# Loading q, k and v as f32 from SP's hardware queue and rounding them to bf16 by copies on Pool, in a dilated sliding-window attention with soft mixture of experts

## The chip, the cores and the metric

One core of one Trainium2 chip runs the whole kernel. The metric is the device time of one launch in microseconds (us). Engines are named as in the profile: PE (TensorE), PEld (its weight loads), DVE (VectorE), ACT (ScalarE), POOL (GpSimd), SP (SyncE, which only issues DMAs here). Fewer microseconds are better.

## The reference

Eight batches (B = 8) of eight heads (H = 8), 576 positions (S), head width 64 (D). The first four heads of a batch look back over the last 32 positions, the other four over the last 128 at every fourth position. The result, 4608 tokens of width 512, goes through a soft mixture of experts with 8 experts of 4 slots each.

```python
scores = scale * np.matmul(q, k.transpose(0, 1, 3, 2))
mask_plain = (rel >= 0) & (rel < 32)
mask_dil   = (rel >= 0) & (rel < 32 * 4) & (rel % 4 == 0)
attn = softmax(np.where(masks, scores, -1e9))          # rows
x = (attn @ v) as (4608, 512)
logits = x @ phi                                       # (4608, 32)
d = softmax(logits over tokens); slot_input = d.T @ x  # (32, 512)
slot_out[e] = relu(slot_input[e] @ w1[e]) @ w2[e]      # w1[e] 512x1024, w2[e] 1024x512
out = softmax(logits over slots) @ slot_out            # (4608, 512)
```

q, k, v, the weights and the output are f32 in HBM; the kernel computes in bf16 with f32 sums.

## The kernel before, in words

**Units.** The work is cut into 16 units n (`NSU`): one batch and one half of its heads, even units the plain window, odd units the dilated one. Each unit takes three loads, k, q and v of four heads (w = 3n, 3n + 1, 3n + 2), 48 loads in all, each 128 partitions by 1152 elements. A unit runs through stages: `stage_T` (L632) transposes k, q and v on PE (L640 in even units, L643 in odd ones) and ACT or DVE copies them out of PSUM into `seq`, in the tile `aren` (helper `cp`, L330 for ACT, L331 for DVE); `stage_V` (L656) transposes blocks of v (L672); `stage_S` (L687) puts the mask into PSUM by a matmul (L695, L698) and adds the scores (L704); `stage_P` (L714) takes row maxima on DVE (L723), splits them into a bf16 head and a bf16 rest by a small subtraction on DVE (L725), subtracts both on PE (L732), takes exp on ACT (L738) and transposes (L745); `stage_O` (L754) multiplies with v (L766) and divides (L776, L778); `stage_X` (L782) transposes the result (L796). Every second unit `gating` (L810) adds a batch to the gate's running sums.

**Loads.** `load(w)` (L472) brings one load in two halves of 64 partitions (`NPQ = 2`). The DMAs are issued on Pool's software queue (L485) and round f32 to bf16 on their way. They land in a ring of 9 slots (`NSLOT`, 1152 elements each) in the tile `stg_all`; load w goes into slot w mod 9, and so can't start before the transposes of load w - 9 are done. Pool's queue also issues the weights (`load_w`, L489, L504): w1 and w2 of the 8 experts in four pieces each, 64 DMAs, rounded on their way too. Six experts' w2 have a place of their own (`N_W2R = 6`, tile `w2b`); experts 6 and 7 reuse `stg_all` when its slots are done. phi comes on SP's hardware queue (L553), and so does the output at the end (L1132, 19 DMAs). Pool has little else: selects that build the identity (L513), the masks (L524, L527, L547) and the group mask `mskg` (L584, L588) in the first 25 us.

**After the units.** The gate's sums are closed (L998 to L1020), `slot_input` is formed (L1022, L1030), the first layer runs (`first_layer`, L1037, matmuls L1043), the hidden values are transposed (L1062), the second layer runs (`second_layer`, L1070, matmuls L1076), and then 36 blocks of the output are multiplied (L1117), copied (L1125 on ACT, L1126 on DVE) and stored.

**What sets the order.** Every operation is given to a planner (`Prog`): with the engines that may run it and a cost in us, what it reads and writes (`Buf`) and a priority (`P.cur`). `schedule` (L161) goes through time by those costs: of the operations ready on an engine it takes the one of best priority, and it picks ACT or DVE where both may do. The order so found is fixed for each engine, and `emit` (L242) writes it out with semaphore waits where an operation needs another engine's result (or, on Pool, always the operation before it). So a changed cost or engine changes the whole order. An operation marked `paced` (most loads, all weights) waits, besides, for the landing of an earlier load, so chosen that about 3 us of transfers (`COVER`) stand ahead of it. Loads of unit n + 3 get priority 100n - 100, weights 1700 (a lower number goes first).

```python
for n in range(NSU):
    P.cur = 100 * n - 60
    stage_T(n)
    P.cur = 100 * n - 100
    for w in range(3 * n + NSLOT, min(3 * n + NSLOT + 3, 3 * NSU)):
        load(w)
```

Of the kernel before, what the change touches and what calls it, by code (L numbers as in the profile page):

```python
# [19 lines left out]
LSEQ = 2 * S  # L20
# [82 lines left out]
class Op:  # L103
    __slots__ = ("opts", "fn", "raw", "war", "prio", "rounds", "eng", "start", "end",
                 "sem", "val", "clock", "hard", "mm", "bytes", "dsem", "nleft", "users", "idx", "waits", "paced",
                 "more")


class Prog:
# [12 lines left out]
    def op(self, opts, fn, r=(), w=(), a=(), rounds=(), prio=None, dma=None, extra=(), hard=(), mm=1,  # L122
           paced=False):
        o = Op()
        o.paced = paced
        o.mm = mm
        o.more = self.more
        o.idx = len(self.ops)
        o.opts, o.fn = opts, fn
        o.prio = self.cur if prio is None else prio  # L130
        o.rounds = list(rounds)
        o.bytes, o.dsem = dma if dma else (0, None)
        raw, war = set(extra) | set(hard), set()
        o.hard = set(hard)
        for b in r:
            raw.update(b.w)
        for b in a:
            war.update(b.prev)
        for b in w:
            raw.update(b.w)  # L140
            war.update(b.prev)
            war.update(b.r)
        for b in r:
            b.r.append(o)
        for b in a:
            b.w.append(o)
        for b in w:
            b.prev = b.w + b.r
            b.w, b.r = [o], []
        for rd in o.rounds:  # L150
            rd.ops.append(o)
            if len(rd.ops) > 1:
                raw.update(rd.ops[:-1])
        raw.discard(o)
        war.discard(o)
        o.raw, o.war = raw, war - raw
        o.eng = None
        self.ops.append(o)
        return o

    def schedule(self):  # L161
# [22 lines left out]
        while ready:  # L184
# [43 lines left out]
            if o.bytes:  # L228
                dma_free = max(dma_free, o.end + 1.3) + o.bytes / 400e3
                o.end = dma_free + 0.4  # L230
                if e == "POOL":
                    loads.append((o, o.bytes / 400e3))
# [9 lines left out]
    def emit(self, nc, blk):  # L242
# [6 lines left out]
        for o in self.order:  # L249
# [7 lines left out]
            for d in o.war:  # L257
                if d.dsem is None and d.eng == e:
                    continue
                need.append(d)  # L260
# [73 lines left out]
def bass_dilated_sliding_attn__then__soft_moe_slots_kernel(  # L334
# [16 lines left out]

    NSLOT = 9
    SLOT = 1152
    w1b = sb("w1b", [128, E_EXP, 4, FF])
    N_W2R = 6
    w2b = sb("w2b", [128, N_W2R, 8, DM])
    stg_all = sb("stg_all", [128, NSLOT * SLOT])
    slots = [stg_all[:, SLOT * i:SLOT * (i + 1)] for i in range(NSLOT)]
    VW = 18 * 2 * 66
# [44 lines left out]

    sm_all = stg_all[:, 8192:9408].bitcast(F32)
    sab = sm_all[:, 0:256].bitcast(BF16)
# [19 lines left out]

    b_stg = [Buf() for _ in range(NSLOT)]
    b_seq = [[Buf() for _ in range(3)] for _ in range(2)]
    b_VOV = [Buf() for _ in range(2)]
# [22 lines left out]
    NPQ, NPW = 2, 4  # L452
    s_stg = [[nc.alloc_semaphore(f"s_stg{i}_{j}") for j in range(NPQ)] for i in range(NSLOT)]
    s_w1 = [[nc.alloc_semaphore(f"s_w1_{e}_{j}") for j in range(NPW)] for e in range(E_EXP)]
# [17 lines left out]
    def load(w, paced=True):  # L472
        n, t = w // 3, w % 3
        b, ty = su_bt(n)
        i = w % NSLOT
        hs = (k, q, v)[t][b, 4 * ty:4 * ty + 4]
        if ty == 0:
            dst = slots[i].rearrange("p (h c) -> p h c", h=2)
            ap = hs.rearrange("(p x) (i c) d -> (x i) p (c d)", p=2, c=9)
        else:  # L480
            dst, ap = slots[i], hs.rearrange("h (i c) d -> (h i) (c d)", c=18)
        m = 128 // NPQ
        for j in range(NPQ):
            sl = slice(m * j, m * j + m)
            P.op(POOL, lambda g, sl=sl: g.dma_start(dst[sl], ap[sl]),  # L485
                 dma=(m * LSEQ * 5, s_stg[i][j]), paced=paced,
                 **(dict(w=[b_stg[i]]) if j == 0 else dict(a=[b_stg[i]])))

    def load_w(kk, e):  # L489
# [6 lines left out]
        for i in range(n_p):  # L496
# [4 lines left out]
            else:  # L501
                sl = (slice(m * i, m * i + m), slice(0, c))
                bw = b_w
            P.op(POOL, lambda g, sl=sl: g.dma_start(dst[sl], ap[sl]), paced=True,  # L504
                 dma=(4 * DM * FF // n_p, sem[i]),
# [4 lines left out]
    small(lambda vv: vv.memset(ident[:], 0.0), w=[b_ident])  # L510
    for w in range(3):
        load(w, False)
    pool(lambda g: g.affine_select(  # L513
        out=ident[:], in_=ident[:], compare_op=AluOp.not_equal, fill=1.0, base=0,
        pattern=[[-1, 128]], channel_multiplier=1), w=[b_ident], r=[b_ident])

    for w in (3, 4):
        load(w, False)
    for i in range(2):
# [10 lines left out]
    for j in range(1, 4):  # L530
        small(lambda vv, j=j: vv.tensor_copy(mbase[32 * j:32 * j + 32, :], mbase[0:32, :]),
              w=[b_mb], r=[b_mb])
    for w in range(5, NSLOT):
        load(w)
    small(lambda vv: vv.tensor_scalar(idneg[:], ident[:], -1.0, None, op0=AluOp.mult),
# [414 lines left out]
    for n in range(NSU):  # L950
        P.more = P.DVE_MORE if n < NSU - 1 else 0.0
        P.cur = 100 * n - 60
        stage_T(n)
        P.cur = 100 * n - 100
        for w in range(3 * n + NSLOT, min(3 * n + NSLOT + 3, 3 * NSU)):
# [17 lines left out]
    P.more = 0.0  # L973
    stg_of = lambda c0, c1: [b_stg[i] for i in range(c0 // SLOT, min((c1 - 1) // SLOT + 1, NSLOT))]
    for i, e in enumerate(range(N_W2R, E_EXP)):
# [13 lines left out]
    for nb in (b_sab, b_siT, b_rep, b_frow):  # L989
        for bb in stg_of(8192, 9408):  # L990
            nb.r += bb.all_ops()
# [189 lines left out]
```

## Time and profile before

| | |
|---|---|
| median of 3 runs | 234.81 us (234.13 to 240.28) |
| the profiled execution, its own time | 232.67 us |
| its span, first to last instruction | 230.9 us |
| mean granted TensorE clock | 0.901 |
| first transposes of k | 5.59 us |
| loads of q, k, v issued | 1.3 to 134.8 us |
| weights issued | 48.7 to 196.4 us |
| first layer's matmuls begin | 191.15 us |
| output stores issued | 204.4 to 224.4 us |

A line of the page's first part gives an engine's busy time, its share of the span and its instructions. In the groups and in the timeline, "out<-in" names the tiles; "idle before" in square brackets is how long the engine had nothing to do and what ended that. The waits add such idle times up by who waited for whom: total us, times, longest. The chain is followed back from the last instruction, at each step to what released it. A PE that is busy is not a PE at its peak, since matmuls overlap; the granted clock is the share of the full TensorE clock in that stretch.

```
stretch (us)   PE busy  DVE busy  ACT busy  POOL busy  granted clock  DMA share
12 to 20        7.71      3.89      5.39      6.79        1.00          1.02
20 to 40       16.17     14.53     12.39     11.18        1.00          0.96
60 to 80       18.14     13.12     11.54      7.39        0.85          0.87
120 to 140     17.32     13.71     11.88      8.44        0.91          0.96
160 to 180     15.49     11.68      8.52      6.54        0.83          0.98
190 to 200      9.16      4.76      0.00      2.66        0.72          0.99
207 to 231      9.41     13.38      8.48      0.00        0.76          0.92
```

### The profile page before, as it was taken

The numbers are of one execution on the slowest core, as the hardware profiler recorded it, in microseconds if no ns is written. First come the engines' busy times: TensorE is split into PE (matmuls) and PEld (weight loads), VectorE is DVE, ScalarE is ACT, GpSimd is POOL, SyncE is SP. The second block draws the span as 40 slices with busy tenths as digits, with TensorE's granted clock in tenths as the row PEclk, the third lists the DMA queues.
The fourth block names the chain that finished last, engine by engine and source line by source line (L and its number), as shares of the span: only waits on it lengthen the run. The fifth ranks groups of instructions, "written<-read, shape, count | busy, mean of one in ns | idle before, by whom it ended". The sixth has DMA issues, their size and how long they took to land.

```text
span 230.9 us, 9919 instructions
## 1 busy us (share of the span) xinstructions
PE 181.4 (79%) x4502; PEld 123.9 (54%) x4502; DVE 145.5 (63%) x322; ACT 121.9 (53%) x190; POOL 89.3 (39%) x187
## 2 busy tenths in 40 slices
PE   0699597996999899899789979698969479984810
PEld 0476476665767568566556657366744343442300
DVE  3356586788547667677785676728772463468750
ACT  2557665864538779674685748264634120073640
POOL 7687564434506444542544343233341333000000
PEclk9999999999779999999997999979985755999785
DMA  6999998799987999999989899979999899849996
GB/s 85 179 142 163 156 153 124 112 163 137 157 170 101 148 168 162 150 161 173 158 136 174 165 168 160 189 136 193 186 183 193 138 169 177 143 177 406 397 408 253
DMA packets 17562, 41.08 MB, mean 178 GB/s; under 512 B 3440, under 2 KB 9584, under 8 KB 15600
## 3 DMA queue, kind: packets, MB, share of 16 engines
q0 software_dynamic: 14208, 30.94, 80.9%
q1 hardware_dynamic: 3312, 9.50, 10.6%
q8 instruction: 35, 0.57, 1.0%
q14 instruction: 7, 0.06, 0.1%
HBM read 61.93 MB, written 9.44 MB: 309 GB/s over the span
## 4 chain that ended last, share of the span: by engine, by line
PE 64%; DVE 12%; issue 8%; ACT 6%; DMA 5%; POOL 1%; SPq 0%; DVEq 0%; POOLq 0%
PE ps L672 9%; PE ps L732 7%; PE ps L640 6%; PE ps L704 5%; PE ps L766 4%; PE ps L745 4%; PE ps L796 4%; PE ps L695 4%; PE ps L643 4%; DVE aren L331 3%; DMA out_dram<-aren 3%; DVE aren L1126 3%; PE ps L1043 3%; DMA stg_all<-in_v_dram 2%; ACT aren L330 2%
## 5 line engine op out<-in xcount | busy, mean ns | idle before, releaser
L330 ACT ACTIVATE aren<-ps 128x1152 bf16<-128x1152 bf16 (+2 forms) x49 | 53.0, 1099 | 34.0 <-PE ps L640 12.4
L331 DVE COPY aren<-ps 128x1152 bf16<-128x1152 bf16 (+2 forms) x31 | 34.2, 1113 | 10.9 <-PE ps L640 4.7
L723 DVE TENSOR_REDUCE nm<-ps 128x10 f32<-128x640 f32 (+1 forms) x32 | 24.1, 753 | 7.1 <-PE ps L704 6.8
L504 POOL DMA_DIRECT2D w1b<-in_moe_w_dram x32 | 15.9, 497 | 27.3 <-DMA w1b<-in_moe_w_dram 10.0
L485 POOL DMA_DIRECT2D stg_all<-in_k_dram x32 | 17.9, 562 | 21.6 <-PE ps L640 12.6
L778 DVE TENSOR_TENSOR xn<-ps,rv 128x576 bf16<-128x576 f32 x32 | 24.2, 758 | 1.1
L640 PE MATMUL ps<-ident,stg_all 128*64 128x128 bf16 x432 | 18.4, 243 | 7.5 <-DMA stg_all<-in_k_dram 5.6
L672 PE MATMUL ps<-ident,aren 128*128 128x128 bf16 (+1 forms) x304 | 22.7, 232 | 1.8 <-issue 1.5
L485 POOL DMA_DIRECT2D stg_all<-in_v_dram x32 | 17.7, 558 | 14.4 <-DMA stg_all<-in_k_dram 5.3
L330 ACT ACTIVATE xt<-ps 128x640 bf16<-128x640 bf16 (+1 forms) x21 | 13.2, 661 | 18.9 <-PE ps L796 18.8
L738 ACT ACTIVATE pp<-ps 128x640 bf16<-128x640 f32 (+1 forms) x32 | 20.0, 654 | 4.7 <-PE ps L732 4.2
L766 PE MATMUL ps<-aren,pp 64*32 64x65 bf16 x1152 | 15.2, 194 | 8.8 <-issue 6.7
L504 POOL DMA_DIRECT2D w2b<-in_moe_w_dram x24 | 11.7, 489 | 26.3 <-DMA w2b<-in_moe_w_dram 22.1
L485 POOL DMA_DIRECT2D stg_all<-in_q_dram x32 | 17.7, 560 | 9.9 <-PE ps L643 3.0
L640 PEld LDWEIGHTS ps<-ident,stg_all 128*64 128x64 bf16 x432 | 15.1, 124 | 11.1 <-POOL ident L513 5.6
L672 PEld LDWEIGHTS ps<-ident,aren 128*128 128x128 bf16 (+1 forms) x304 | 18.3, 105 | 3.4 <-issue 1.8
L704 PE MATMUL ps<-aren 64*32 64x64 bf16 x1152 | 15.7, 196 | 3.7 <-issue 3.7
L704 PEld LDWEIGHTS ps<-aren 64*32 64x32 bf16 x1152 | 11.5, 95 | 12.5 <-issue 12.5
L766 PEld LDWEIGHTS ps<-aren,pp 64*32 64x32 bf16 x1152 | 10.9, 92 | 13.2 <-issue 7.6
L643 PE MATMUL ps<-ident,stg_all 128*128 128x128 bf16 x216 | 16.4, 223 | 2.0 <-issue 1.6
L732 PE MATMUL ps<-nm,idneg 128*128 128x512 bf16 (+1 forms) x48 | 16.4, 352 | 0.1
L643 PEld LDWEIGHTS ps<-ident,stg_all 128*128 128x128 bf16 x216 | 13.2, 100 | 4.6 <-issue 1.9
(143 smaller groups left out, 311.4 us busy)
## 6 DMA issues: line engine op xcount, KB each, us to landing
out_dram<-aren SPq DMA_DIRECT2D x17, 512.0 KB, 5.6
w1b<-in_moe_w_dram POOLq DMA_DIRECT2D x32, 256.0 KB, 5.6
w2b<-in_moe_w_dram POOLq DMA_DIRECT2D x24, 256.0 KB, 5.6
stg_all<-in_k_dram POOLq DMA_DIRECT2D x32, 144.0 KB, 4.3
stg_all<-in_q_dram POOLq DMA_DIRECT2D x32, 144.0 KB, 4.7
stg_all<-in_v_dram POOLq DMA_DIRECT2D x32, 144.0 KB, 4.7
stg_all<-in_moe_w_dram POOLq DMA_DIRECT2D x8, 256.0 KB, 5.5
out_dram<-aren SPq DMA_DIRECT2D x2, 256.0 KB, 2.3
```

The costliest lines, as they stand in the source:

```text
L330: return eng.activation(dst, src, ACTF.Copy)
L331: return eng.tensor_copy(dst, src)
L485: P.op(POOL, lambda g, sl=sl: g.dma_start(dst[sl], ap[sl]), dma=(m * LSEQ * 5, s_stg[i][j]), paced=paced, **(dict(w=[b_stg[i]]) if j == 0 ...
L504: P.op(POOL, lambda g, sl=sl: g.dma_start(dst[sl], ap[sl]), paced=True, dma=(4 * DM * FF // n_p, sem[i]), **(dict(w=[bw]) if i == 0 or bw ...
L640: ins = pe_.transpose(rd.h[64 * p:64 * p + 64, oc], sl[:, 576 * p + 64 * c:576 * p + 64 * c + 64], ident[:])
L643: ins = pe_.transpose(rd.h[:, oc], sl[:, oc], ident[:])
L672: ins = pe_.transpose(rd.h[row:row + nk, 128 * i:128 * i + 128], seq[u][:, 2, sl], ident[:])
L704: ins = pe_.matmul(rd.f[32 * j:32 * j + 32, 64 * (tile - t0):64 * (tile - t0) + 64], qk(u, p_, k, j, 1, 32, 0), qk(u, p_, k, j, 0, 64, 1), ...
L723: P.op([dve(ne)], lambda vv, sv=sv, nv=nv: vv.tensor_reduce(nv, sv(), AXX, AluOp.max), rounds=[rd], w=[b_nm[u][i]])
L732: ins = pe_.matmul(rd.f[:, 64 * a:64 * b], idneg[:], m[:, a:b].unsqueeze(2).to_broadcast([128, b - a, 64]), start=False, stop=True, skip_g ...
L766: ins = pe_.matmul(rd.f[32 * oq:32 * oq + 32, 103 * pl:103 * pl + 65], pt[u][sl, tile // 2, 32 * j:32 * j + 32], VOV[u][sl, pv, j % 2 if u ...
L778: P.op([dve(576)], lambda vv, cols=cols, rvp=rvp, p=p: vv.tensor_tensor(xn[x][:, :, p, :], cols(0, 64), rvp.unsqueeze(2).to_broadcast([128 ...
```

## The change

The 96 half loads of q, k and v are issued on SP's hardware queue. They are not rounded on their way: they land as f32 in a ring of 5 f32 slots (`NFS`, load w in slot w mod 5). A copy on Pool for each load (48, given to the planner at 1.2 us) rounds it into one of 4 bf16 slots (load w in slot w mod 4), which `stage_T` reads as before. A load waits for the copy of load w - 5, a copy for its load and for the transposes of load w - 4. The weights stay on Pool's queue and are still rounded on their way; they are issued among the copies. `stg_all` grows from 9 x 1152 to 14 x 1152 elements of two bytes, and `w2b` shrinks from 6 experts to 5, so that experts 5, 6 and 7 reuse `stg_all` at the end. The loads' priority becomes 100n - 200, and only the first 4 loads stand ahead of the loop in the program. The order of every engine is planned anew. On SP the first six half loads stand ahead of phi's four DMAs. On Pool the order at the start is: a weight issue, the select for the identity, a weight issue, two selects for `mbase`, two for `mask`, the first copy, five selects, the second copy, a select, the third copy.

```diff
-    NSLOT = 9
+    NSLOT, NFS = 4, 5
     SLOT = 1152
-    N_W2R = 6
+    N_W2R = 5
-    stg_all = sb("stg_all", [128, NSLOT * SLOT])
-    slots = [stg_all[:, SLOT * i:SLOT * (i + 1)] for i in range(NSLOT)]
+    stg_all = sb("stg_all", [128, (2 * NFS + NSLOT) * SLOT])
+    fslots = [stg_all[:, 2 * SLOT * i:2 * SLOT * (i + 1)].bitcast(F32) for i in range(NFS)]
+    slots = [stg_all[:, SLOT * i:SLOT * (i + 1)] for i in range(2 * NFS, 2 * NFS + NSLOT)]
...
-        i = w % NSLOT
+        i = w % NFS
...
-            dst = slots[i].rearrange("p (h c) -> p h c", h=2)
+            dst = fslots[i].rearrange("p (h c) -> p h c", h=2)
...
         for j in range(NPQ):
             sl = slice(m * j, m * j + m)
-            P.op(POOL, lambda g, sl=sl: g.dma_start(dst[sl], ap[sl]),
-                 dma=(m * LSEQ * 5, s_stg[i][j]), paced=paced,
+            P.op([("SP", 0.6)], lambda sp, sl=sl: sp.dma_start(dst[sl], ap[sl]), load=True,
+                 dma=(int(m * LSEQ * 4.5), s_stg[i][j]), paced=paced,
...
+        P.op([("POOL", 1.2)], lambda g: g.tensor_copy(slots[w % NSLOT], fslots[i]),
+             r=[b_fst[i]], w=[b_stg[w % NSLOT]])
...
-    for w in range(3):
-        load(w, False)
+    for w in range(NSLOT):
+        load(w, w > 2)
...
-    for w in (3, 4):
-        load(w, False)
...
-    for w in range(5, NSLOT):
-        load(w)
...
-        P.cur = 100 * n - 100
+        P.cur = 100 * n - 200
```

The rest of the diff adapts the planner (it counts DMAs marked `load` for the pacing, instead of those on Pool; a weight DMA on Pool waits for a Pool copy that still uses its place) and moves the small tiles that share `stg_all` from column 8192 to 12288.

More of the change, by code (lines that the diff above doesn't have):

```diff
@@ L105 @@
                  "sem", "val", "clock", "hard", "mm", "bytes", "dsem", "nleft", "users", "idx", "waits", "paced",
-                 "more")
+                 "more", "load")
 class Prog:
@@ L122, in op @@
     def op(self, opts, fn, r=(), w=(), a=(), rounds=(), prio=None, dma=None, extra=(), hard=(), mm=1,
-           paced=False):
+           paced=False, load=False):
         o = Op()
+        o.load = load
         o.paced = paced
@@ L230, in schedule @@
                 o.end = dma_free + 0.4
-                if e == "POOL":
+                if o.load:
                     loads.append((o, o.bytes / 400e3))
@@ L257, in emit @@
             for d in o.war:
-                if d.dsem is None and d.eng == e:
+                if d.dsem is None and d.eng == e and (e != "POOL" or o.dsem is None):
                     continue
@@ L403, in bass_dilated_sliding_attn__then__soft_moe_slots_kernel @@
     last = sb("last", [128, 1], F32)
-    sm_all = stg_all[:, 8192:9408].bitcast(F32)
+    sm_all = stg_all[:, 12288:13504].bitcast(F32)
     sab = sm_all[:, 0:256].bitcast(BF16)
@@ L427, in bass_dilated_sliding_attn__then__soft_moe_slots_kernel @@
     b_stg = [Buf() for _ in range(NSLOT)]
+    b_fst = [Buf() for _ in range(NFS)]
     b_seq = [[Buf() for _ in range(3)] for _ in range(2)]
@@ L452, in bass_dilated_sliding_attn__then__soft_moe_slots_kernel @@
     NPQ, NPW = 2, 4
-    s_stg = [[nc.alloc_semaphore(f"s_stg{i}_{j}") for j in range(NPQ)] for i in range(NSLOT)]
+    s_stg = [[nc.alloc_semaphore(f"s_stg{i}_{j}") for j in range(NPQ)] for i in range(NFS)]
     s_w1 = [[nc.alloc_semaphore(f"s_w1_{e}_{j}") for j in range(NPW)] for e in range(E_EXP)]
@@ L474, in load @@
         b, ty = su_bt(n)
-        i = w % NSLOT
+        i = w % NFS
         hs = (k, q, v)[t][b, 4 * ty:4 * ty + 4]
         if ty == 0:
-            dst = slots[i].rearrange("p (h c) -> p h c", h=2)
+            dst = fslots[i].rearrange("p (h c) -> p h c", h=2)
             ap = hs.rearrange("(p x) (i c) d -> (x i) p (c d)", p=2, c=9)
         else:
-            dst, ap = slots[i], hs.rearrange("h (i c) d -> (h i) (c d)", c=18)
+            dst, ap = fslots[i], hs.rearrange("h (i c) d -> (h i) (c d)", c=18)
         m = 128 // NPQ
@@ L484, in load @@
             sl = slice(m * j, m * j + m)
-            P.op(POOL, lambda g, sl=sl: g.dma_start(dst[sl], ap[sl]),
-                 dma=(m * LSEQ * 5, s_stg[i][j]), paced=paced,
-                 **(dict(w=[b_stg[i]]) if j == 0 else dict(a=[b_stg[i]])))
+            P.op([("SP", 0.6)], lambda sp, sl=sl: sp.dma_start(dst[sl], ap[sl]), load=True,
+                 dma=(int(m * LSEQ * 4.5), s_stg[i][j]), paced=paced,
+                 **(dict(w=[b_fst[i]]) if j == 0 else dict(a=[b_fst[i]])))
+        P.op([("POOL", 1.2)], lambda g: g.tensor_copy(slots[w % NSLOT], fslots[i]),
+             r=[b_fst[i]], w=[b_stg[w % NSLOT]])
     def load_w(kk, e):
@@ L503, in load_w @@
                 bw = b_w
-            P.op(POOL, lambda g, sl=sl: g.dma_start(dst[sl], ap[sl]), paced=True,
+            P.op(POOL, lambda g, sl=sl: g.dma_start(dst[sl], ap[sl]), paced=True, load=True,
                  dma=(4 * DM * FF // n_p, sem[i]),
@@ L973, in bass_dilated_sliding_attn__then__soft_moe_slots_kernel @@
     P.more = 0.0
-    stg_of = lambda c0, c1: [b_stg[i] for i in range(c0 // SLOT, min((c1 - 1) // SLOT + 1, NSLOT))]
+    seg = [(2 * SLOT * i, 2 * SLOT * (i + 1), b_fst[i]) for i in range(NFS)]
+    seg += [(SLOT * (2 * NFS + i), SLOT * (2 * NFS + i + 1), b_stg[i]) for i in range(NSLOT)]
+    stg_of = lambda c0, c1: [bb for a0, a1, bb in seg if a0 < c1 and c0 < a1]
     for i, e in enumerate(range(N_W2R, E_EXP)):
@@ L989, in bass_dilated_sliding_attn__then__soft_moe_slots_kernel @@
     for nb in (b_sab, b_siT, b_rep, b_frow):
-        for bb in stg_of(8192, 9408):
+        for bb in stg_of(12288, 13504):
             nb.r += bb.all_ops()
```

## The prediction

> **What bounds the kernel now.** I read the page first, for the shares of the engines and queues and for the chain that ended last; then the waits, to see who waits for loads; then the timelines of the start and of one softmax step, because those are the places where the change puts an operation in front of something.
>
> ```profile
> PE 181.4 (79%) x4502; PEld 123.9 (54%) x4502; DVE 145.5 (63%) x322; ACT 121.9 (53%) x190; POOL 89.3 (39%) x187
> ...
> q0 software_dynamic: 14208, 30.94, 80.9%
> q1 hardware_dynamic: 3312, 9.50, 10.6%
> q8 instruction: 35, 0.57, 1.0%
> ...
> PE 64%; DVE 12%; issue 8%; ACT 6%; DMA 5%; POOL 1%; SPq 0%; DVEq 0%; POOLq 0%
> ```
>
> The DMA engines look full (q0 alone 80.9%), but the chain holds 5% of DMA, and the output's stores are 2.6 of that 5. PE, with what feeds it, sets the end. The waits say the same:
>
> ```profile
> POOL stg_all L485 <- PE ps L640: 14.1, 8, 4.2
> ...
> PE ps L640 <- DMA stg_all<-in_k_dram: 5.6, 1, 5.6
> ...
> PE ps L640 <- DMA stg_all<-in_q_dram: 1.5, 1, 1.5
> ...
> PEld ps L1076 <- DMA stg_all<-in_moe_w_dram: 0.2, 1, 0.2
> ```
>
> PE waits for k and q once each, at the very start, and never again: in the loop it is the loads that wait for PE to free a slot (14.1 us in 8 waits). For the last expert weights it waits 0.2 us. So there is no DMA wait in the loop for faster loads to remove. What is left is the start:
>
> ```profile
> 5.59 1.17 PE L640 MATMUL ps<-ident,stg_all 128*64 128x128 bf16 x18 [5.59 <-DMA stg_all<-in_k_dram]
> 8.25 1.17 PE L640 MATMUL ps<-ident,stg_all 128*64 128x128 bf16 x18 [1.49 <-DMA stg_all<-in_q_dram]
> 9.70 1.17 PE L640 MATMUL ps<-ident,stg_all 128*64 128x128 bf16 x18 [0.28 <-DMA stg_all<-in_v_dram]
> 10.81 0.61 PE L695 MATMUL ps<-mask,ident 128*128 128x512 bf16 x1
> ```
>
> The first unit's k, q and v are transposed at 5.59, 8.25 and 9.70 us, and the first scores start at 10.81. From there PE has little rest (7.71 of the 8 us from 12 to 20).
>
> **The change, part by part.**
>
> *The loads' issue.* 96 loads leave Pool's queue: 96 x 0.56 us (the L485 groups, 53.3 us in all) of a Pool that is busy 39%. They go to SP, where one issue of such a half takes about 0.6 us (the four phi loads, 2.66 us together). Pool's time was not on the chain (1%), so this gains nothing by itself. On SP they stand ahead of the four phi loads, which move from 0.80 to about 4.4 us (six issues of 0.6). phi landed at 7.7, so now at about 11.3; its copy on DVE stands right ahead of the first score maximum, which came at 12.24 and comes later now: hidden, with some 2 us of cover.
>
> *The transfers.* q, k and v are 14.16 MB of the 30.94 MB on q0, 85.5 of its 186.8 us (80.9% of 230.9) by bytes. As f32 they are 28.3 MB on a hardware queue; the nearest row is q1, 9.50 MB in 24.5 us (10.6%), 388 GB/s, mostly output stores: 73.0 us. So the 16 engines do 12.5 us less. On the path lies only the 0.2 us wait for the last weights: gain 0.2.
>
> *The copies.* 48 copies of 128x1152 from f32 to bf16 on Pool. The trace has none. The nearest rows on Pool:
>
> ```profile
> 5.08 0.29 POOL L513 TENSOR_SCALAR_AFFINE_SELECT ident<-ident 128x128 bf16<-128x128 bf16 x1
> ...
> 7.40 0.29 POOL L524 TENSOR_SCALAR_AFFINE_SELECT mbase<-mbase 32x64 bf16<-32x64 bf16 x1
> ...
> 8.79 0.18 POOL L584 TENSOR_SCALAR_AFFINE_SELECT mskg<-mskg 32x1 f32<-32x1 f32 x1
> ```
>
> From one column to 128 costs 0.11 us, 0.87 ns a column: 0.18 + 1152 x 0.87 ns = 1.2 us. From one to 64 costs the same 0.11, 1.75 ns a column: 2.2 us. I take 1.2 (that row has the full 128 partitions and is the longest) and keep 2.2. Pool then has 48 x 1.2 + 68 weight issues x 0.49 = 91 us, as much as its 89.3 now: not a bound.
>
> *The start.* The new order on Pool is: weight issue, select for ident, weight issue, two selects for mbase, two for mask, first copy, five selects, second copy, one select, third copy. With issues of 0.72 and 0.5 and selects at a pitch of 0.3 to 0.43, mbase is ready at 3.75; DVE's chain from mbase to mask took 1.33 us (8.92 to 10.25), so the two mask selects end at about 6.0. k has landed by then or soon after: its second half took about 2.9 us from issue to landing before, and 2.1 + 2.9 is 5.0, plus up to 1.3 for a weight transfer beside it. First copy 6.0 to 7.2; five selects, 1.7 us; second 8.9 to 10.1; third 10.4 to 11.6. v's transposes move from 9.70 to 11.6: +1.9 us. With copies of 2.2 the third ends at 14.6: +4.9. PE has no slack behind this point, so I carry +1.9 to the end. Later copies have 11 us per unit for three (3.6 us), and each runs as soon as the transposes four loads back are done: hidden.
>
> *What waits behind the copies on Pool.* Each copy waits for its load and for a bf16 slot; the weight issues stand behind it. Before, loads waiting for PE held the weights up in the same way. After the last copy there are 20 weight issues, at the 1.38 us of the last 32 (153.7 to 196.4 us) 28 us. The last copy needs unit 14's q, transposed before about 154: 182, with 5.5 to land 188, against 202 when PE uses the last ones. Cost nothing; the cover is 14 us. Experts 5 to 7 now share the staging: the f32 slots are free at the last copy, the bf16 slot one unit from the end: no wait.
>
> *DVE beside the copies.* Pool now reads SBUF for 57.6 us of about 150. DVE's small subtraction (L725, 32 of them) stands between the maximum and PE:
>
> ```profile
> 96.82 0.16 DVE L725 TENSOR_TENSOR nl<-nm 128x10 bf16<-128x10 f32 x1
> ...
> 97.04 0.10 PEld L732 LDWEIGHTS ps<-nm,idneg 128*128 128x128 bf16 x1 [0.27 <-DVE nl L725]
> 97.04 0.39 PE L732 MATMUL ps<-nm,idneg 128*128 128x512 bf16 x1
> ```
>
> Here PE starts 0.06 us after the subtraction ends. By the timeline, 7 of the 32 have such a gap of 0.06 or less, 3 about 0.24, 14 about 0.52, and 8 have 0.75 or more. If a copy held the subtraction until it ended, each would be hit with 0.38 (57.6/150) and wait evenly up to 1.2 us, and PE would lose what exceeds the gap: 0.38 x (7 x 0.56 + 3 x 0.38 + 14 x 0.19) = 3.0 us. With 2.2 us (0.70; 1.06, 0.87, 0.64) 13.3. The other bound is nothing: the nearest row shows no hold.
>
> ```profile
> 8.50 0.22 POOL L588 TENSOR_SCALAR_AFFINE_SELECT mskg<-mskg 32x1 f32<-32x1 f32 x1
> 8.50 0.39 DVE L576 TENSOR_TENSOR sel<-sel,ident 128x32 bf16<-128x32 bf16 x2
> ```
>
> Two DVE operations with two SBUF inputs run beside a select at 0.2 us each; but the select reads one column. Between 0 and 3.0 I take the middle, +1.5. [...]
>
> *Sum.* +1.9 (start) + 1.5 (DVE) - 0.2 (last weights) = +3.2 on the profiled execution's 232.67 us (span 230.9): 235.9. That execution lies 2.1 under the median of the three runs, 234.81, so against it: 238.0.
>
> **Rivals.** (B) The copies take longer and DVE is held: at 1.7 us the start costs 3.4 (three copies of 0.5 more) and the holds 7.2 (0.54 x 13.3 by the same sum), +10.4 and 245.2; at 2.2 us, 4.9 + 13.3 - 0.2 = 18.0, 252.8. It passes 2% (4.7 us, about what a measurement of this kernel can tell from no change) from a copy of some 1.3 us with full holds. For it: the 32x64 select's price; against it: the 128x128 one's. (C) Faster: relief of the DMA engines shortens PE's "issue" time, 8% of the chain, 18.5 us, through the instruction queue q8. If 40% went, -7.4 + 1.9 - 0.2 = -5.7: 229.1. It needs 6.4 us to pass -2%. For it: DMA shares of 0.9 to 1.0 all through the loop; against: a q8 packet takes 1.06 us on average (1.0% of 16 x 230.9 over 35), and the longest such wait (2.5 us, at 148.15) comes among weight loads alone, which stay. [...] (D) No change: nothing is held and the start is made up: 234.6. (E) Weights late: copies waiting for PE hold the weight issues by more than the 14 us of cover; 19 us late gives +5 beyond the rest, 243.
>
> **How the numbers follow.** Forecast 0.40 (its own range 234 to 242, about a third of it above 239.5), B 0.30, C 0.17, D 0.08, E 0.05. Faster by over 2%: 0.17. Slower by over 2%: 0.30 + 0.05 + 0.12 = 0.47. Within: 0.36. The range from 230 to 248 leaves out the far halves of B (copies near 2.2) and of C, about a tenth on each side.
>
> **What would show it.** Start: v's first transposes at 11.6 in PE's timeline, waiting for Pool. Copies: their mean near 1.2 us. DVE: L725's row (now 147/162/171 ns) stretched, or an idle time ahead of it, beside copies. Loop: no waits of PE for Pool's copies but the first three. Last weights: landing before 200, no wait for them. Wrong if the copies take 2 us or more, if PE waits for copies in the loop, or if PE's "issue" share moves by more than 2 points.

## The result and the profile after

The changed kernel takes 260.73 us (median of 6 runs, 256.24 to 261.61) against 234.47 us (6 runs, 231.81 to 240.28): a ratio of 1.106, 95% interval 1.087 to 1.125. It is slower by 26 us, against +3.2 forecast and a range that ended at 248. Here and below a time is the median of all runs, with the lowest and the highest, while a ratio takes only the faster runs of each kernel, since executions of one kernel differ by some per cent.

The profiled execution of the changed kernel took 260.39 us, with a span of 258.6 at a granted clock of 0.904 (before: 230.9 at 0.901, so the clock explains none of the 27.7 us between these two). Its page, with the same lines as were shown of before: engines, queues, chain.

```profile
PE 180.5 (70%) x4475; PEld 127.2 (49%) x4502; DVE 152.4 (59%) x321; ACT 120.7 (47%) x191; POOL 91.1 (35%) x139
...
q1 hardware_dynamic: 14064, 37.82, 55.0%
q0 software_dynamic: 3456, 16.78, 36.3%
q8 instruction: 35, 0.57, 1.0%
...
PE 33%; DMA 28%; DVE 14%; issue 12%; POOL 5%; ACT 4%; SPq 1%; POOLq 0%; DVEq 0%
```

PE does as much work as before (180.5 us against 181.4; 27 of its records are missing) in a longer span. The chain has changed: DMA from 5% to 28%, PE from 64% to 33%, "issue" from 8% to 12%. The DMA engines have more to do, not less: q1 takes 142.2 us of them (55.0% of 258.6), q0 93.9, together 236.1; before it was 24.5 + 186.8 = 211.3. The 236.1 us are more than the kernel before lasts (230.9). The packets of q, k and v alone, those of 2304 and 4608 bytes on q1, took 116.5 us in the trace.

Now who waits, in the waits of the whole span (total us, times, longest):

```profile
POOL w1b L511 <- DMA stg_all<-in_q_dram: 33.6, 10, 8.0
...
PE ps L706 <- issue: 14.5, 13, 2.5
PE ps L642 <- POOL stg_all L493: 14.4, 4, 8.4
...
PE ps L645 <- POOL stg_all L493: 5.0, 2, 4.6
```

PE now waits for Pool's copies, 19.4 us in six waits, where before it waited for loads at the start alone. The first three of these waits are the start, in PE's timeline:

```profile
8.37 1.17 PE L642 MATMUL ps<-ident,stg_all 128*64 128x128 bf16 x18 [8.37 <-POOL stg_all L493]
12.13 1.17 PE L642 MATMUL ps<-ident,stg_all 128*64 128x128 bf16 x18 [2.59 <-POOL stg_all L493]
14.89 1.17 PE L642 MATMUL ps<-ident,stg_all 128*64 128x128 bf16 x18 [1.59 <-POOL stg_all L493]
```

k, q and v are transposed 2.8, 3.9 and 5.2 us later than before. The other 6.9 us of waits for copies lie in the loop. The copies are not to blame themselves: they start at 16.40, 18.87 and 21.35 us, 2.5 us apart, and take 1.15. One load of 590 KB in 2.5 us is 236 GB/s, and the page's row of GB/s stands at 234 and 237 in these slices. It is the loads that come late.

Adding up PE's waits by what ended them, from 10 to 215 us: 30.9 us before, 51.3 after. Of the 20.4 more, 11.0 end with a copy on Pool (4.2 of them at the start), 9.8 with "issue" (14.8 to 24.6), 3.0 with ACT, and those for DVE fall by 3.1, those for DMA by 0.3. The division of unit 0 comes 6.6 us later than before, that of unit 1 13.2, of unit 4 21.5, of unit 5 13.9 (the two kernels order the units' steps differently), of unit 8 24.8, of unit 10 25.3, of unit 15 28.8: most of the loss builds up in the first half of the loop.

### The profile page after: what moved, and what is told of

The parts are those of the page before. It is cut to its first block, busy times and chain, and to the rows that moved or that the text cites. A ratio compares the mean times of both kernels' runs of the same rounds, so it can differ in the third digit from the quotient of the medians.

```text
span 258.6 us, 9980 instructions
## 1 busy us (share of the span) xinstructions
PE 180.5 (70%) x4475; PEld 127.2 (49%) x4502; DVE 152.4 (59%) x321; ACT 120.7 (47%) x191; POOL 91.1 (35%) x139
## 4 chain that ended last, share of the span: by engine, by line
PE 33%; DMA 28%; DVE 14%; issue 12%; POOL 5%; ACT 4%; SPq 1%; POOLq 0%; DVEq 0%
DMA stg_all<-in_q_dram 8%; DMA w1b<-in_moe_w_dram 7%; DMA stg_all<-in_v_dram 6%; DMA stg_all<-in_k_dram 5%; POOL stg_all L493 5%; DVE aren L332 3%; PE ps L674 3%; PE ps L706 3%; PE ps L734 3%; PE ps L645 3%; PE ps L798 3%; PE ps L642 3%; DVE xn L780 3%; DMA out_dram<-aren 2%; DVE aren L1130 2%
## 5 line engine op out<-in xcount | busy, mean ns | idle before, releaser
L331 ACT ACTIVATE aren<-ps 128x1152 bf16<-128x1152 bf16 (+2 forms) x49 | 49.6, 1024 | 55.1 <-PE ps L642 20.9
L493 POOL CAST stg_all<-stg_all 128x1152 bf16<-128x1152 f32 x48 | 55.3, 1153 | 17.8 <-issue 5.2
L332 DVE COPY aren<-ps 128x1152 bf16<-128x1152 bf16 (+2 forms) x31 | 36.1, 1168 | 20.1 <-PE ps L645 9.5
L706 PE MATMUL ps<-aren 64*32 64x64 bf16 x1152 | 17.5, 197 | 15.7 <-issue 14.5
L642 PEld LDWEIGHTS ps<-ident,stg_all 128*64 128x64 bf16 x432 | 15.4, 126 | 19.4 <-POOL stg_all L493 15.3
L780 DVE TENSOR_TENSOR xn<-ps,rv 128x576 bf16<-128x576 f32 x32 | 24.2, 757 | 1.1
L331 ACT ACTIVATE xt<-ps 128x640 bf16<-128x640 bf16 (+1 forms) x19 | 12.5, 673 | 23.2 <-PE ps L798 23.1
L645 PE MATMUL ps<-ident,stg_all 128*128 128x128 bf16 x216 | 18.1, 241 | 5.5 <-POOL stg_all L493 5.0
L645 PEld LDWEIGHTS ps<-ident,stg_all 128*128 128x128 bf16 x216 | 15.6, 111 | 9.2 <-issue 6.8
L674 PEld LDWEIGHTS ps<-ident,aren 128*128 128x128 bf16 (+1 forms) x304 | 17.4, 102 | 4.5 <-issue 2.0
L331 ACT ACTIVATE pp<-ps 128x1152 bf16<-128x1152 bf16 x12 | 13.5, 1129 | 13.0 <-PE ps L747 13.0
L511 POOL DMA_DIRECT2D w2b<-in_moe_w_dram x20 | 9.8, 492 | 19.6 <-DMA w2b<-in_moe_w_dram 10.8
L747 PE MATMUL ps<-ident,pp 128*128 128x128 bf16 x144 | 13.5, 224 | 3.7 <-issue 2.1
```

Of the source, the lines that this page charges most:

```text
L331: return eng.activation(dst, src, ACTF.Copy)
L332: return eng.tensor_copy(dst, src)
L493: P.op([("POOL", 1.2)], lambda g: g.tensor_copy(slots[w % NSLOT], fslots[i]), r=[b_fst[i]], w=[b_stg[w % NSLOT]])
L642: ins = pe_.transpose(rd.h[64 * p:64 * p + 64, oc], sl[:, 576 * p + 64 * c:576 * p + 64 * c + 64], ident[:])
L645: ins = pe_.transpose(rd.h[:, oc], sl[:, oc], ident[:])
L674: ins = pe_.transpose(rd.h[row:row + nk, 128 * i:128 * i + 128], seq[u][:, 2, sl], ident[:])
```

## The experiments

The base is named with each. The runs fall into four groups, each on another chip, and the kernel before was run again beside each (medians of 7 to 13 runs): 235.33 us for the loads by themselves, the column halves and the planner's figure; 236.61 for the first runs of the pace, of the held weights, of the copies on other engines and of the idle copies; 235.46 for their second runs; 237.04 for the two kernels that part transfers and order and for the two with short copies. Times of different groups are best compared by their ratios to the kernel before.

### The loads by themselves

Twelve loads of q, k and v are moved five times over, one way after the other, with nothing else in the kernel (it computes nothing, and its output is zeros): as f32 from SP in halves of 64 partitions; as f32 from SP in halves of 576 columns over 128 partitions; rounded on Pool's queue in both forms; as f32 on Pool's queue in halves of 64 partitions.

> This kernel computes nothing of the reference: it loads units 0 to 3 (12 loads, 7.08 MB of f32 in HBM) five times, each stretch after the one before has landed, and stores zeros. Stretch 1: f32 on SP's queue, halves of 64 partitions, as the change does it. Stretch 2: the same as halves of 576 columns over all 128 partitions. Stretch 3: rounded to bf16 on Pool's queue, halves of 64 partitions, as before. Stretch 4: that with column halves. Stretch 5: f32, not rounded, on Pool's queue, halves of 64 partitions. Theory A (an f32 half that lands on 64 partitions is written at a limited rate, about the 235 GB/s of the changed kernel's first 40 us): stretch 1 some 30 us, 2 some 18 (388 GB/s, the output's rate), 3 and 4 alike at some 22 (315 GB/s of f32 read, the kernel before from 10 to 20 us), 5 some 30. Theory B (the hardware queue, or f32 as such, is slow): 1 and 2 alike at 30; with the queue at fault 5 takes 18 to 22, with f32 at fault 30.

The five stretches (columns: stretch, its length, busy time and count of DVE and Pool, granted clock, DMA share, GB/s counted as written):

```profile
2.00:31.00 29.00, 15.42 (x1) 0.00 (x0) 1.00 1.03 243
33.00:53.40 20.40, 0.00 (x0) 0.00 (x0) 1.00 0.97 347
56.00:75.50 19.50, 0.00 (x0) 11.88 (x22) 1.00 1.08 181
77.90:97.50 19.60, 0.00 (x0) 11.43 (x22) 1.00 1.13 181
99.80:130.30 30.50, 0.00 (x0) 11.89 (x22) 1.00 1.02 232
```

The same 7.08 MB take 29 us as f32 in partition halves, from either queue (243 and 232 GB/s), and 20 us in column halves. The rounded loads take 19.5 either way: they read the same 363 GB/s but write 181. So neither the hardware queue nor f32 as such is slow, and neither is reading HBM in this pattern; f32 written to 64 partitions at a time is. And the best f32 can do, 20 us, is no better than the rounded load: there was no DMA time to be saved. The rounded halves write 181 GB/s, less than the 232 to 243 of the f32 halves; what sets the f32 halves' rate, and whether it would hold the rounded ones too, no run shows.

### Column halves in the changed kernel, and in the kernel before

The one line that cuts a load in two; queues, order and planner stay.

```diff
-            sl = slice(m * j, m * j + m)
+            sl = (slice(0, 128), j) if ty == 0 else (slice(0, 128), slice(576 * j, 576 * j + 576))
```

> The changed kernel with each load cut into two halves of 576 columns over all 128 partitions instead of two of 64 partitions; the order of every engine, the number of DMAs and their bytes stay the same. Theory A: the 2304-byte packets of q1 fall from 154 ns to about 95, the first 14 copies on Pool follow each other at 1.6 us instead of 2.5, PE's waits for Pool's copies (20 us) go, and the time falls from 260 to 236 to 242 us. Theory B: nothing moves, 256 to 262. Theory C (Pool's order: weight issues that wait for a paced landing stand in front of the copies): some of the waits stay, 248 to 256.

> The kernel before with column halves over 128 partitions, order unchanged: the control of the cut. Theory A: rounded to bf16, a half writes half the bytes, so 64 partitions did not limit it: 233 to 237 us, no change. If cutting by columns helped here too (below 231), the cut would be worth something by itself and the comparison of e2 had to be made against this kernel.

The changed kernel falls from 260.7 to 248.65 us (244.67 to 251.7; ratio to before 1.054, 1.037 to 1.071). Before with the same cut stays: 235.42, ratio 1.007 (1.000 to 1.015). So 12 us of the 26 are the halves' landing. In the waits of the changed kernel with column halves, PE's waits for copies are down from 19.4 to

```profile
PE ps L642 <- POOL stg_all L493: 11.3, 3, 9.2
```

and all three are the start, the first of 9.2 and these two:

```profile
12.15 1.17 PE L642 MATMUL ps<-ident,stg_all 128*64 128x128 bf16 x18 [1.82 <-POOL stg_all L493]
13.61 1.17 PE L642 MATMUL ps<-ident,stg_all 128*64 128x128 bf16 x18 [0.29 <-POOL stg_all L493]
```

In the loop PE waits for no copy any more. The copies are hidden, and 13 us of loss remain. The next runs look for those.

### The planner's figure for a load, and the pace

The plan thinks of a half as 0.83 us of transfer, and of a load as twice that; it takes 2.5. First, told the truth (base: the changed kernel):

```diff
-                 dma=(int(m * LSEQ * 4.5), s_stg[i][j]), paced=paced,
+                 dma=(int(m * LSEQ * 6.8), s_stg[i][j]), paced=paced,
```

> The changed kernel with the planner told what a half load really takes (1.25 us of transfer instead of 0.83), so that orders and pacing are planned for the measured rate; the transfers are not changed. Theory C: the waits of PE for Pool's copies vanish and the time falls below 250 us. Theory A: the DMA engines still need 48 x 2.5 us for q, k, v and some 87 us for the weights, 207 us before the second layer can end, with 30 us behind it: 248 to 262 us.

272.31 us (270.8 to 276.2; ratio 1.162, 1.149 to 1.175), worse by 12. It moves the weights from the third on from 47.5 to 115.8 us, and PE waits for the last ones, once for 18.1 and once for 10.1 us:

```profile
PE ps L1080 <- DMA stg_all<-in_moe_w_dram: 18.1, 1, 18.1
...
PE ps L642 <- POOL stg_all L493: 11.2, 2, 8.4
...
PE ps L1080 <- DMA w2b<-in_moe_w_dram: 10.1, 1, 10.1
```

The two waits for copies that are left are at the start. In the loop there is none, as the theory of the wrong figure had it, and the division of unit 15 comes 11.9 us later than before instead of 28.8. But the weights pay for it, and that theory's time, under 250, is far off; the other theory missed the time too, since it did not see the weights move. With the slow halves the plan can have the loads in time or the weights; so the wrong figure by itself is not the fault.

Then the pace, taken off SP's loads (`paced=False`), first on column halves, later on the better version of the next section:

> Base: the column-halves kernel (248.65 us). Edit: the loads of q, k and v on SP no longer wait for the planner's pace; only a free f32 slot holds them back (weights keep their pace). Theory Q (in the changed program two queues share one pace: SP's next load waits for a weight's landing, 33.0 us of SP's waits, and Pool's next weight, with the copies behind it, waits for a load's landing, some 44 us; taking SP out of it frees the loads): 244 to 246 us. Theory H or S: 247.5 to 250 us, since PE's waits for the copies in the loop are only some 2 us. Rival: loads run ahead and push the weights back: 250 to 255 us.

> Base: column halves with the weights held at the start (239.15 us). Edit: SP's loads are no longer paced. Theory H (what remains is VectorE's holds): 238 to 240.5 us. Rival Q (the shared pace of two queues still costs some us): 235 to 237 us.

243.52 us (233.66 to 246.6) and 241.51 (239.5 to 243.71). The first is some 5 us better than its base of 248.65, but with runs 13 us apart it shows nothing; the second (ratio 1.027, 1.014 to 1.041) is not better than its base of 239.15 (1.014). In the better version the two queues' common pace isn't what is lost.

### The weights at the head of Pool's queue

In the kernel before, the first weight is issued at 48.7 us. In the changed one the first two stand at the head of Pool's queue, at 1.3 and 2.3 us, and the third at 47.5: no load stands ahead of them in the plan for the pace to hold them. Here every weight waits for the sixth copy, once with column halves, once with the 64-partition halves of the changed kernel.

```diff
-            P.op(POOL, lambda g, sl=sl: g.dma_start(dst[sl], ap[sl]), paced=True, load=True,
+            P.op(POOL, lambda g, sl=sl: g.dma_start(dst[sl], ap[sl]), paced=True, load=True, extra=[copies[5]],
```

> Base: the column-halves kernel (248.65 us). Edit: every weight transfer waits for the sixth rounding, so that nothing but q, k and v is moved while the pipeline fills, and Pool's first copies are not queued behind a weight. Theory S (the late start is what remains: the first transposes of v come 3.9 us later than in before, and the lag that the first units build up is never made good): 244 to 246 us, first v transposes 1 to 2 us earlier, the rest of the lag unchanged. Theory H (holds and queue coupling in the loop): no more than 1 us better than 248.65. Rival W (the weights are pushed back and land late): 249 to 253 us with PE waiting for the last weights.

> Base: the changed kernel (260.7 us). Edit: every weight transfer waits for the sixth rounding, as in the run that gave 239.15 with column halves; the loads stay the 64-partition halves of the changed kernel. Theory L (the two losses are separate: loads at 240 GB/s cost some 12 us by themselves, the two weights ahead of them some 9): 249 to 254 us, transposes of v first at 12 to 13, PE still waiting some 10 us for roundings in the loop. Rival S (the start sets all that follows; with it mended the slow loads find slack): 239 to 244 us. Rival G (the slow loads are all; the start was only where it showed): 258 to 262 us.

With column halves 239.15 us (238.12 to 240.81; ratio 1.014, 1.004 to 1.024): 9.5 us better, far more than any theory had (by the ratios 1.054 and 1.014, 9.3 us). The granted clock was 0.875 to 0.877 in three of the four runs of the base and 0.890 to 0.900 here; how much of the 9.5 us goes with that was not looked into. With 64-partition halves 256.77 (253.36 to 257.5; ratio 1.090, 1.072 to 1.108): only 4 better, between the theories. In this order the slow landing costs 256.77 - 239.15 = 17.6 us.

The first transposes with column halves and held weights, in PE's timeline, nearly those of before:

```profile
5.73 1.17 PE L644 MATMUL ps<-ident,stg_all 128*64 128x128 bf16 x18 [5.73 <-POOL stg_all L495]
8.50 1.17 PE L644 MATMUL ps<-ident,stg_all 128*64 128x128 bf16 x18 [1.60 <-POOL stg_all L495]
10.44 1.17 PE L644 MATMUL ps<-ident,stg_all 128*64 128x128 bf16 x18 [0.77 <-POOL stg_all L495]
```

But holding the weights does two things: it clears the way for the first loads, and it makes the planner lay out another order on every engine. Two kernels part these. One keeps the good order to the last instruction of PE, DVE, ACT and SP and puts two 256 KB weight transfers back at Pool's head; the other keeps the bad order and sends only 4 KB in each of those two places (the whole slices after the sixth copy).

```diff
+    for i in range(2):
+        sl = (slice(32 * i, 32 * i + 32), slice(0, 4))
+        P.op([("POOL", 0.01)], lambda g, sl=sl: g.dma_start(
+            w1b[:, 0][sl], moe_w1[0].rearrange("(p c) f -> p c f", c=4)[sl]),
+            dma=(1, s_first[i]), **(dict(w=[b_w1[0]]) if i == 0 else dict(a=[b_w1[0]])))
```

> Base: column halves with the weights held at the start (239.15 us). Edit: the order of work on every engine stays exactly that of the base, but two 256 KB weight transfers are put at the head of Pool's queue, where the changed kernel has its first two (the same slices are sent again in their turn). Theory T (the two transfers delay the first loads, and the lag stays): 242 to 246 us, first copy 2 to 3 us later. Theory O (with the weights planned first the planner lays out another order of transposes, scores and copies on PE for the whole loop, and it is that order that costs): 239 to 241 us, the late start made good within the first units.

> Base: the column-halves kernel (248.65 us). Edit: the order on PE, VectorE, ScalarE and SP stays exactly that of the base; the two weight transfers at the head of Pool's queue move only 4 KB each, and the whole slices are sent after the sixth rounding. Theory T: 242 to 246 us, the first copy at 5 us instead of 8. Theory O: 246.5 to 249 us, with the start early and the lag growing again by unit 4.

With the transfers back in the way, q and v are late again:

```profile
5.84 1.17 PE L651 MATMUL ps<-ident,stg_all 128*64 128x128 bf16 x18 [5.84 <-POOL stg_all L496]
12.31 1.17 PE L651 MATMUL ps<-ident,stg_all 128*64 128x128 bf16 x18 [5.30 <-POOL stg_all L496]
14.25 1.17 PE L651 MATMUL ps<-ident,stg_all 128*64 128x128 bf16 x18 [0.77 <-POOL stg_all L496]
```

and yet the time is 240.44 us (237.56 to 241.19), by the medians 1.3 more than without them; by the ratio, 1.029 (1.012 to 1.046) against 1.014, it is 3.5 more. The bad order with a clear start takes 245.02 (237.7 to 246.75), 3.6 less than with them; one of its four runs took 237.7, at a granted clock of 0.924, the others 244.8 to 246.8 at 0.878 to 0.898. So by the medians, of the 9.5 us the transfers are 1.3 to 3.6, and the order laid out around them 5.9 to 8.2 (245.02 - 239.15 and 248.65 - 240.44). By the ratios of the two kernels with the transfers, 1.054 in the bad order and 1.029 in the good one, the order is 5.8 us, but their intervals overlap. In the bad order the transposes of unit 2's k come right behind unit 1's v (23.3 us, with unit 2's v at 31.8); in the good one, as in before, the three stand close together (25.7, 26.2, 29.8; before 24.8, 25.3, 29.0). That both the transfers and the order cost something is likely; how the 9.5 us divide between them is not settled. Nor is it shown that the good order makes up for a late start: with the transfers v is transposed 3.8 us later, unit 4 divided 1.8 and unit 15 3.7 us later, and the profiled execution's span is 3.0 us longer (239.4 against 236.4).

### Copies on other engines

The 48 roundings go to DVE or ACT, as the planner chooses, with the weights at Pool's head and with the weights held.

```diff
-        P.op([("POOL", 1.2)], lambda g: g.tensor_copy(slots[w % NSLOT], fslots[i]),
+        P.op([("DVE", 0.75), act(1152)], lambda eng: cp(eng, slots[w % NSLOT], fslots[i]),
```

> Base: the column-halves kernel (248.65 us median; its ratio to before 1.054). Edit: the 48 roundings are done by VectorE or ScalarE, as the planner chooses, instead of Pool; loads, halves and order as in the column-halves kernel. Theory H (Pool's copies hold VectorE's operations on two SBUF sources, and Pool's in-order queue couples weights, copies and loads; both go when the copies leave Pool): 240 to 245 us, no L727 above 0.3 us, PE's waits for L727 back under 0.5 us, although VectorE and ScalarE get some 35 to 50 us more work between them. Rival V (the roundings are work that some engine on the critical path must do; VectorE is already 59% busy in the changed kernel): 248 to 256 us. Rival S (only the start and the landing of the loads count): within 2 us of 248.65.

> Base: column halves with the weights held at the start (239.15 us). Edit: the roundings go from Pool to VectorE or ScalarE, as the planner chooses; Pool keeps weights and selects alone. It settles what the 257.3 us of the same edit without the held weights meant. Theory V (the roundings are work on engines that share the path: some 40 us of it on two engines that are both over half busy): 247 to 255 us. Rival S (that run was bad for its start alone; without Pool's copies the holds are gone): 235 to 238 us.

257.31 us (251.41 to 260.82) and 257.76 (253.46 to 261.32; ratio 1.086, 1.065 to 1.108), worse than 248.65 and 239.15. In the second kernel the groups read:

```profile
L331 ACT ACTIVATE stg_all<-stg_all 128x1152 bf16<-128x1152 f32 x33 | 38.2, 1164 | 23.4 <-PE ps L644 11.7 <-PE ps L647 5.3 <-DMA stg_all<-in_k_dram 3.9
L332 DVE CAST stg_all<-stg_all 128x1152 bf16<-128x1152 f32 x15 | 11.3, 757 | 8.6 <-PE ps L644 3.5 <-PE ps L647 3.2 <-DMA stg_all<-in_k_dram 1.8
```

49.5 us of rounding, and 32 us of idle time ahead of it, on two engines that PE needs for every other step: Pool was the right engine of the three.

### What Pool's copies do to DVE

A hold, as one step of it looks in the changed kernel (timeline, all engines):

```profile
21.35 1.15 POOL L493 CAST stg_all<-stg_all 128x1152 bf16<-128x1152 f32 x1 [1.07 <-DMA stg_all<-in_v_dram]
21.44 1.07 DVE L727 TENSOR_TENSOR nl<-nm 128x8 bf16<-128x8 f32 x1
...
22.62 0.38 PE L734 MATMUL ps<-nm,idneg 128*128 128x512 bf16 x1
```

The small subtraction takes 0.16 us; here it begins 0.09 us into a copy, ends at 22.51 when the copy does (22.50), and PE's matmul comes behind it. In the changed kernel L727 took 0.162 us on average in the 23 cases without a copy and 0.705 in the 9 beside one; DVE operations that read PSUM have the same mean in the kernels before and after (the maxima 753 and 752 ns, L778 and L780 758 and 757). The prediction had such a hold as an "if" ("*If a copy held the subtraction until it ended*"); these rows show it. How much time does it cost? First, copies that nobody needs are put into the kernel before: 43 of 1152 f32 columns from a constant tile into a scratch tile, one for each load from the sixth on.

```diff
+        if w >= 5:
+            P.op([("POOL", 1.2)], lambda g: g.tensor_copy(idle[:], idle_f[:]),
+                 r=[b_idf], w=[b_idle], extra=[landed[w - 5]])
```

> Base: the kernel before (235.3 us). Edit: 43 copies of 1152 f32 elements a partition to bf16 are added on Pool, one for each load from the sixth on, from a constant tile into a scratch tile that nobody reads; the cast loads stay. Theory H (the copies cost what they hold up: VectorE's operations on two SBUF sources, at some 0.5 us each where they meet, on a path that VectorE shares): 3 to 6 us slower, 238 to 241 us, with L727 beside a copy over 0.6 us. Rival N (VectorE makes the holds good, the loss of the changed kernel is all in loads and start): within 1.5 us of 235.3, holds there but no PE wait. Rival P (a copy on Pool delays the issue of a load behind it): over 242 us, with transposes waiting for stg_all's DMAs.

264.9 us (263.1 to 265.1; ratio 1.121, 1.111 to 1.131). None of the theories had it: the planner, seeing Pool full, put the first weight at 129 us instead of 48.7, and PE waited 25 us for the last ones. At the division of unit 15 the kernel was only 3.7 us behind. So the copies were entered at 0.01 us, and in a second kernel of the same order shortened to 64 columns:

> Base: the kernel before (236.6 us in the last call). Edit: the same 43 idle roundings on Pool as in the last run, but entered in the plan at 0.01 us each, so that the weights keep their places in Pool's order (in the run with 264.9 us the planner moved the first weight from 48.7 to 129 us, and 25 us of waits for weights followed). Theory H (the holds on VectorE cost some 3 to 4 us in the loop, as the lag of 3.7 us at the last unit of that run says): 238.5 to 241.5 us, no wait for weights over 2 us. Rival N (the lag was the planner's, the holds cost nothing): 235.5 to 237.5. Rival P (copies in Pool's queue delay loads and weights): over 242 us.

> Base: the kernel before with 43 idle roundings on Pool (249.8 us; VectorE 160.3 us busy against 145.5). Edit: same order on every engine; each idle rounding covers 64 of the 1152 columns. Theory H (the length of the copies does it: holds on VectorE, and Pool occupied): 235.5 to 238.5 us, VectorE near 146. Rival P (43 more entries in Pool's order, their waits, and the plan laid out around them do it): 246 to 250 us.

249.81 us (248.8 to 250.02; ratio 1.065, 1.055 to 1.074) and 236.79 (235.04 to 240.08; 1.015, 1.000 to 1.030). Same order on every engine, 13 us apart (12 by the ratios). The engines of the long copies, and then of the short ones:

```profile
PE 188.3 (76%) x4502; PEld 127.5 (51%) x4502; DVE 160.3 (65%) x323; ACT 122.8 (49%) x190; POOL 137.0 (55%) x230
```

```profile
PE 187.0 (78%) x4502; PEld 128.5 (54%) x4502; DVE 146.8 (62%) x323; ACT 122.4 (51%) x190; POOL 98.8 (41%) x230
```

DVE's time differs by 13.5 us with the same work: held time counts as busy. Pool's time differs too, by 38 us, and with it the moment at which it issues what stands behind a copy: the last load goes out at 152.55 us with the long copies and at 138.61 with the short ones. PE waits 2.0 us for the subtraction with the long copies and 2.2 for transfers after the start, and for neither with the short ones. So the pair shows that the copies' length costs 12 to 13 us in this kernel, and not how much of that is the holds. Here the copies stand behind DMA issues on Pool, and a hold may begin during the issue and last to the copy's end. Two steps of the kernel with the long copies (timeline of DVE; the copies run from 85.99 to 87.15 and from 109.30 to 110.48, behind issues of 0.6 us):

```profile
85.76 1.42 DVE L734 TENSOR_TENSOR nl<-nm 128x8 bf16<-128x8 f32 x1
...
108.83 1.69 DVE L734 TENSOR_TENSOR nl<-nm 128x10 bf16<-128x10 f32 x1
```

The same test in the good version of the change: from the fifth load on, its copies round only 64 of the 1152 columns (so it computes with old values).

```diff
-            lambda g: g.tensor_copy(slots[w % NSLOT], fslots[i])
+            lambda g, c=1152 if w < NSLOT else 64: g.tensor_copy(slots[w % NSLOT][:, 0:c], fslots[i][:, 0:c])
```

> Base: column halves with the weights held at the start (239.15 us). Edit: same order on every engine; from the fifth load on Pool rounds only 64 of a load's 1152 columns (the rest of each bf16 slot keeps old values, so the output is not the reference's). That takes away the copies' length and nearly all of their holds on VectorE. Theory H (the rest of the loss, 1.4%, is the holds): VectorE's busy time falls by 4 to 5 us to 146, time 235 to 237 us. Rival N (the holds are made good, the rest lies elsewhere, as in the start or the f32 transfers): 238 to 240 us.

241.07 us (237.09 to 243.69) against 239.15 (238.12 to 240.81): no gain, though DVE's time falls from 150.3 to 146.3 us. In this kernel, 4 us of holds cost nothing that the runs, 6.6 us apart, can show; in the kernel with the idle copies 13.5 us of them, and a fuller Pool, come with 12 to 13 us of time. Why the one is absorbed and the other not was not settled.

## Why the prediction was wrong, step by step

- **The transfers, the step that failed.** (The forecast's +3.2 had the sign right, but not for this reason: it came from the start and from holds on DVE.) "*The nearest row is q1 ... 388 GB/s, mostly output stores*", hence 73.0 us for the 28.3 MB of q, k and v and 12.5 us of DMA time saved, with nothing of it on PE's path. That row holds stores from 128 partitions; the loads land in 64 at a time, and their packets took 116.5 us. In the loads-alone kernel they move at 243 GB/s, and at 347 in the other form; rounded loads read 363 and had nothing to gain. Engine time of the DMAs rose by 24.8 us instead (211.3 to 236.1). Three loads a unit at 2.5 us are 7.5 us of a unit's 11, before the weights: what had been hidden became a wait. Price: 12.1 us in the changed kernel's order, 17.6 in the better one. Two of the signs of being wrong that the prediction had named came with it: PE waited for copies in the loop, and its "issue" share rose by 4 points.
- **"Later copies ... hidden".** Wrong by consequence: 6.9 us of waits in the loop. With column halves it was right: none.
- **The copies' price** was right: 1.2 forecast, 1.153 us measured. Some of that is luck: it was extrapolated ninefold from a select of 128 columns in bf16, and the other select at hand gave 2.2. So rival B, which needed longer copies, was not the cause, though the time went beyond its figures.
- **The start.** +1.9 forecast, +5.2 measured. The first two weights were named, at up to 1.3 us; with them and the slow halves k's first copy began at 7.17 instead of 6.0, and the third at 13.69 instead of 10.4. Whether "PE has no slack behind this point" holds stays open: in the good order v's transposes 3.8 us later cost 1.3 us by the medians and 3.5 by the ratios.
- **What the step left out.** "The order of every engine is planned anew" stood in the description and got no price. In column halves it is worth 5.9 to 8.2 us by the medians and 5.8 by the ratios, which are not clear of each other.
- **DVE beside the copies.** The sum's "if" was right: a copy holds the subtraction (0.705 us beside one, 0.162 without). The sum put 12 of 32 beside a copy (0.38), and it was 9; it carried 1.5 us, between 0 and 3.0, as PE's loss. L727 was held 4.9 us in all (9 x 0.54), DVE was busy 6.9 us more, and PE itself waited 1.1 us for the subtraction; no run shows that in the changed kernel the holds cost the time.
- **Weights behind the copies**: PE never waited for the last ones, as forecast, but by another way: they were to have landed by 188 us and were issued up to 220.0 (196.4 before), and it did no harm because PE was late as well. (The sum there counts 68 weight issues; there are 64, which changes nothing.)
- **Rival C** had "issue" shrink. It grew from 14.8 to 24.6 us. The gaps of PE over 0.6 us in which a packet of the instruction queue q8 ends, or that begin up to 0.3 us behind its end, grew from 10.0 to 22.3 us, and its packets in the loop from 1.01 to 1.18 us on average; with column halves and held weights they are at 13.7 and 1.01. So the sign was the other way. That q8's packets on busy DMA engines delay PE's instructions is the author's reading of these gaps; no run isolated it.

The sum, by runs: 26.3 us = 12.1 (halves of 64 partitions) + 9.5 (weights at Pool's head: the order they bring about, and their transfers, in shares not settled) + some 2.5 to 4.7 (239.15 against 236.61 beside it, or 234.47). The parts are not independent: mended alone, the weights give 4.0. The last term stays open between holds, f32's doubled bytes and the plan. No version of the change came out faster than the kernel before: the best is 1.4% slower (0.4 to 2.4).

## What to carry to other kernels

Price a transfer by a row with the same number of partitions, the same direction and the same bytes written, not by the queue it is on (here a row of stores at 388 GB/s stood for loads that ran at 243 by themselves); if there is none, move it alone on the chip. A load that rounds on its way may already read as fast as one that doesn't (here 363 GB/s, against 347 for f32 in column halves), and then f32 on another queue saves nothing and adds a copy. Where a planner lays out the order, a moved operation changes more than its own place: hold the order fixed in one experiment before giving its effect to a wait.

## What the runs showed of the hardware that was not expected

- Loads of f32 into 64 partitions at a time ran at 232 to 243 GB/s, from either queue; into 128 partitions at 347. Rounded loads show no such difference (19.5 and 19.6 us).
- On SP, issuing a 64-partition half took about 0.63 us, a column half over 128 partitions mostly 0.45 (1.26 and 0.91 for two).
- A Pool copy from f32 to bf16 takes 1.0 ns a column of 128 partitions (1.153 us for 1152); the same copy takes 0.757 us on DVE and 1.164 on ACT.
- A copy right behind a DMA issue on Pool held a DVE subtraction for up to 1.69 us, from within the issue to the copy's end; beside issues alone it takes its 0.16 us (0.164 on average in 22 cases of the kernel before). What makes the hold begin early was not looked into (spans on Pool are rough).
- The granted clock in runs of the slower kernels was often lower (0.84 to 0.88 in the runs of the plan told the truth, of the held weights with 64-partition halves and of the roundings on DVE and ACT with held weights; 0.875 to 0.93 in those of before). What sets it was not looked into; differences of 2 or 3 us between kernels are not explained here for that reason.
